# Sigmoid attention and a gated FFN on one core: order of sums in late-sum pairs, place of batch 4's re-laying

## The chip, the cores and the metric

One core of a Trainium2 chip. The time is device microseconds of one execution; the kernel before took a median of 389.58 us in 3 runs (389.45 to 390.1). Engines in the profile: PE is TensorE (PEld its weight loads), DVE is VectorE, ACT is ScalarE, POOL is GpSimd, SP is SyncE, which here issues stores and transposing DMAs.

## The reference, cut to what matters

```python
batch, n_heads, seq, head_dim = (8, 12, 448, 64)
n_tokens, d_model, d_ff = (3584, 768, 1536)

def _attn_ref(q, k, v):
    scores = scale * np.matmul(q, k.transpose(0, 1, 3, 2)) - np.log(S)
    attn = 1.0 / (1.0 + np.exp(-scores))
    return np.matmul(attn, v).astype(np.float32)

def _moe_ref(x, w_gate, w_val, w_out):
    gate = np.maximum(x @ w_gate, 0.0)
    val = x @ w_val
    return (gate * val @ w_out).astype(np.float32)
```

The attention's output, heads side by side (3584 x 768), is the x of the second function; the result is 3584 x 768 in float32. Everything comes in and goes out as float32; the kernel computes in float16 with float32 sums.

## The kernel before, in words

**Attention.** A batch (8 of them, 448 tokens each) has three groups of four heads. k and q of a batch are loaded by POOL's queue with a cast to float16 (`load`, L107), v in three pieces (`load_v`, L113). They are re-laid for the scores: `dma_transposes(b, g)` (L218) makes two copies on VectorE into a tile `rel` (L222, one of k, one of q) and one transposing DMA on SP's queue into `qkT` (L226). There is one buffer for a batch's k and one for its q, so the next batch's loads wait until the last of these copies has read them.

A **score unit** (`qk_unit`, L299) is four 64x64 matmuls of 448 columns that run beside each other (L239) into two PSUM banks, and two sigmoids on ScalarE (L187) into `PT`. Seven units make a group; then `pv_group` (L307, matmuls L257) multiplies them with v into two banks, and `put_xT` writes the result to `xT` on VectorE (L184).

**FFN.** Two batches make a group g of 896 tokens. Gate and value of a pair of 128-wide feature blocks come from `gv_pair` (L588): the Strassen-Winograd scheme with seven products (six matmuls of 448 columns each, L380) in place of eight. The order on TensorE is b, c, b, a, b, c, b, where b is bank pair "u", c "g2", a "g1". VectorE and ScalarE take the partial results out: a first copy of b (L628, by `first_copy`, one copy for each of two banks), `copy` of c and b on ScalarE (L614), `plus` on VectorE (L618), and the gating (L623). A product that adds to a bank whose earlier value is still to be copied has to wait for that copy. The weight sums of the next pair (`unit_sums`, L555) and the sums of x (`batch_sums`, L580) are VectorE's work too. The down projection of two 128-token tiles is `down_pair` (L443), again seven products, of 384 columns, with `token_sums` (L419, four VectorE operations of 128x768) for each pair. `FRESH` and `SUMS_LATE` name pairs whose last token sums are made late: (1, 0), (1, 1), (2, 0), (2, 1) and (3, 3); these have an order of products of their own, in which the products on the late sums come later. In these pairs, `amid` issues a burst of score units into the middle of the pair, and `then` makes the sums of the next pair.

**Order.** Nothing is scheduled by a tool: each engine works through its instructions in the order of the program text. The loop over b (from L912) issues bursts of score units (`burst`, at the places given by `cuts`, with the value product of a group at `pv_at`) and after each burst one pair of FFN work (`next_work`, L887), to which it hands jobs: `ahead` run first, `jobs` inside the pair (`beside`), behind `prepare`, which makes the sums of the next pair. In batch 4 six `gv_pair` of group 1 follow six bursts; in batch 5 come (1, 0), (1, 1), (1, 2); (2, 0) and (2, 1) close batch 7. In batch 4 the first pair (m == 0) also has the sums of x (`batch_sum_steps`) on VectorE, ahead of the first copies and behind the weight sums.

**Banks.** `bank()` (L77) hands out the eight PSUM banks in a ring; `later` (L85) moves some to the ring's end. A matmul into a bank waits until the bank's last reader is done.

Of the kernel before, what the change touches and what calls it, by code (L numbers as in the profile page):

```python
# [18 lines left out]
def kernel(  # L19
# [10 lines left out]
    nc = tc.nc  # L30

    B, H, S, D = q.shape
# [3 lines left out]
    P = 128  # L36
# [48 lines left out]
    def later(order):  # L85
        keys = [free[i - 8] for i in order]
        for key in keys:
            free.remove(key)
            free.append(key)
# [260 lines left out]
    def store(g, t, ysb, m0, m1, engines):  # L350
        for i, eng in enumerate(engines):
            j = 2 * t + i
            b, c = 2 * g + j // NCH, j % NCH
            dst = out[b * S : (b + 1) * S, m0:m1].rearrange("(t c) m -> c t m", c=NCH)[c]
            eng.dma_start(dst, ysb[64 * i : 64 * i + 64, m0:m1])

    HF, HM, HD = NFC // 2, DM // 2, NDC // 2
# [15 lines left out]
    def sums_tile(inner):  # L373
        S3 = late["sums"].tile([P, 3, HF * P], FP16, tag="S", name="S")
        return [S3[:, i, :].rearrange("p (x y) -> p x y", y=inner) for i in range(3)]
# [21 lines left out]
    FRESH = {1: 0, 2: 0, 3: NPP}  # L397
# [21 lines left out]
    def token_sums(g, p, k0=0, k1=HF):  # L419
        for step in token_sum_steps(g, p, k0, k1):  # L420
            step()
# [21 lines left out]
    def down_pair(g, p, beside, then, last, first_copy, amid=None):  # L443
        A11, A12, S3, A22 = token_blocks(g, p)
        S1, S2, S4 = sums.pop(("y", g, p))
        T1, T2, T3, T4 = late["T"]
        B11, B21, B22 = wo[:, 0:HF, 0:HM], wo[:, HF:NFC, 0:HM], wo[:, HF:NFC, HM:DM]
        y1, y2 = (ysbp.tile([P, DM], FP32, tag="ysb", name="ysb") for _ in range(2))
        lo, hi = slice(0, HM), slice(HM, DM)
        b, c = bank("u"), bank("y12")  # L450
        if not amid or (g, p) in SUMS_LATE:
            a = bank("y11")
            later((7, 6, 5))

        def product(ps, A, W, first=True):
            products([(ps, HM, HF, A, W, first)])

        def plus(o, ps):
            nc.vector.scalar_tensor_tensor(  # L459
                out=o, in0=ps[:, 0:HM], scalar=OUT_SCALE, in1=o, op0=AOP.mult, op1=AOP.add  # L460
            )

        first, second = tiles_in(g, p)

        product(b, A11, B11)
        first_copy(y1[:, lo], b)
        beside()
        if (g, p) in SUMS_LATE:
            product(a, A12, B21)
            plus(y1[:, lo], a)  # L470
            product(c, S1, T1)
            scaled_act(y2[:, hi], c)
            product(b, S2, T2, False)
            scaled_act(y1[:, hi], b)
            product(c, S4, B22, False)
            plus(y1[:, hi], c)
            store(*first, y1, 0, DM, (nc.sync, nc.sync))
            if amid:
                amid()
                then()  # L480
            product(b, S3, T3, False)
            plus(y2[:, hi], b)
            scaled_act(y2[:, lo], b)
            d = bank("y21")
            if amid:
                later((0, 7))
            else:
                then()
            product(d, A22, T4)
            plus(y2[:, lo], d)  # L490
            store(*second, y2, 0, DM, (nc.sync, nc.sync))
            return
        product(c, S1, T1)
        scaled_act(y2[:, hi], c)
        product(b, S2, T2, False)
        scaled_act(y1[:, hi], b)
        if amid:
            product(c, S4, B22, False)
            plus(y1[:, hi], c)
            amid()  # L500
            product(b, S3, T3, False)
            plus(y2[:, hi], b)
            later((0,))
            a = bank("y11")
            later((6,))
            product(a, A12, B21)
            plus(y1[:, lo], a)
        else:
            product(a, A12, B21)
            plus(y1[:, lo], a)  # L510
            if last:
                store(*first, y1, 0, HM, (nc.sync, nc.sync))
            product(b, S3, T3, False)
            plus(y2[:, hi], b)
            if last:
                scaled_act(y2[:, lo], b)
                store(*second, y2, HM, DM, (nc.sync, nc.scalar))
            product(c, S4, B22, False)
            plus(y1[:, hi], c)
        if last:  # L520
            store(*first, y1, HM, DM, (nc.sync, nc.scalar))
        else:
            store(*first, y1, 0, DM, (nc.sync, nc.sync))
        then()
        if last:
            for m0 in (0, HM // 2):
                m1 = m0 + HM // 2
                d = bank("y21")
                products([(d, HM // 2, HF, A22, T4[:, :, m0:m1], True)])
                nc.vector.scalar_tensor_tensor(  # L530
                    out=y2[:, m0:m1], in0=d[:, 0 : HM // 2], scalar=OUT_SCALE, in1=y2[:, m0:m1],
                    op0=AOP.mult, op1=AOP.add,
                )
            store(*second, y2, 0, HM, (nc.sync, nc.scalar))
        else:
            product(b, A22, T4, False)
            scaled_act(y2[:, lo], b)
            store(*second, y2, 0, DM, (nc.sync, nc.sync))
# [13 lines left out]
        yield lambda: gate_sums(f, f + 2)  # L552
        yield from unit_sum_steps(("s", f), f, views)

    def unit_sums(key, f):  # L555
        for step in unit_sum_steps(key, f, sums_tile(2 * P)):
            step()

    def unit_sum_steps(key, f, tiles):
        S1, S2, S4 = tiles  # L560
        fs = slice(f * P, (f + 2) * P)
        A11, A12 = wg[:, 0:HD, fs], wg[:, HD:NDC, fs]
        S3, A22 = wv[:, 0:HD, fs], wv[:, HD:NDC, fs]
        sums[key] = S1, S2, S4
        return (
            lambda: sub(S2, A22, S3),
            lambda: nc.vector.tensor_tensor(out=S1, in0=S2, in1=A11, op=AOP.add),
            lambda: sub(S4, A12, S2),
        )
# [18 lines left out]
    def gv_pair(g, f, beside, first_copy):  # L588
# [3 lines left out]
        b, c, a = ([bank(nm) for _ in range(2)] for nm in ("u", "g2", "g1"))  # L592
# [16 lines left out]
            for u in range(2):  # L609
                products([(ps[u], S, HD, sets[u][i], W, first)])  # L610

        def copy(i, ps, by=nc.scalar.copy):
            for u in range(2):
                by(gs[u][i][:], ps[u][:, 0:S])  # L614

        def plus(i, ps):
            for u in range(2):
# [7 lines left out]
            )  # L625

        product(b, 0, B11)
        copy(0, b, first_copy)  # L628
        product(c, 3, T1)
        copy(2, c)  # L630
        product(b, 4, T2, False)
# [243 lines left out]
            tail.insert(NPP if g == 1 else 0, ("y", g, NPP))  # L875
        work.extend(tail)

    def prepare():
        if work:
            kind, g, i = work[0]  # L880
            if kind == "w":
                unit_sums(("w", g, i), i)
            elif kind == "y":
                if (g, i) != (0, 0):
                    token_sums(g, i, 0, HF - 2 if FRESH.get(g) == i else HF)

    def next_work(jobs=(), alone=False, amid=None, ahead=()):  # L887
        kind, g, i = work.popleft()

        due = pending[:]  # L890
        del pending[:]

        def beside():
            for job in due + list(jobs):
                job()

        for job in ahead:
            job()
        if kind == "y":
            down_pair(g, i, beside, prepare, not work, scaled_act if alone else scaled, amid)  # L900
        elif amid:
            raise ValueError(kind)
        elif kind == "w":
            gv_pair(g, i, lambda: (prepare(), beside()), nc.scalar.copy if alone else nc.vector.tensor_copy)
        elif kind == "s":
            gv_split(g, i, lambda: (prepare(), beside()))
        else:
            gv(g, 0, S, i, True)
            beside()
            prepare()  # L910

    for b in range(1, B):  # L912
        if b == 1:
            cuts, pv_at = (0, 3, 6, 9, 13, 17, 21), {3: (0, 2), 5: (1, 2)}
        else:
            cuts, pv_at = (0, 4, 7, 11, 14, 18, 21), {0: (-1, 1 if b == 4 else 2), 2: (0, 2), 4: (1, 2)}
        bursts = list(range(len(cuts) - 1))
        inner = {}
        if b > 2:
# [31 lines left out]
        for m in range(count):  # L951
            jobs, ahead = [], []
            burst(bursts[m])
            if m == 0 and b > 3:
                jobs.append(lambda: dma_transposes(b, 2))
            if b == 2 and m == 3:
                jobs += [lambda: dma_transposes(3, 0), lambda: dma_transposes(3, 1)]
# [7 lines left out]
            if b == 1:  # L965
                if m == 0:
                    load(2, 0, 1, "kq")
                    load(2, 1, 2, "kq")
                    load(2, 2, 3, "kq")
            elif m == 0 and b + 1 < B:  # L970
                for g0, g1 in ((0, 1), (1, NG)) if b == 3 else ((0, NG),) if b > 3 else ():
                    jobs.append(lambda g0=g0, g1=g1: load(b + 1, g0, g1, "kq"))
                jobs.append(lambda: load_v(b + 1))
# [70 lines left out]
```

## Time and profile before

| | |
|---|---|
| median of 3 runs | 389.58 us (389.45 to 390.1) |
| profiled execution | 390.02 us, span of its instructions 388.1 us |
| PE busy | 381.9 us, 98% |
| DVE busy | 303.3 us, 78% |
| ACT busy | 228.5 us, 59% |
| POOL busy | 49.8 us, 13% |
| granted TensorE clock | 1.000 |

The span runs from the first to the last instruction; the 1.92 us beside it lie outside. Rows of the time order have the start in us from the span's start, the length, the engine, line and operation, output and input, size and count; a bracket at the end gives idle time ahead of the row and what ended it. Rows of equal instructions are merged, and a row's length runs from the start of its first to the end of its last. Each burst of units is a row of `qk_ps` (x4 for one unit), a value product is `pv_ps` x28, a product of an FFN pair x6.

### The profile page before, as it was taken

How to read it: one execution, taken by the hardware profiler on the slowest of the kernel's cores; microseconds unless marked ns; L12 is line 12 of the kernel's file. 1: busy time of each engine (PE TensorE's matmuls, PEld its weight loads, DVE VectorE, ACT ScalarE, POOL GpSimd, SP SyncE). 2: the span in 40 equal slices, each digit the busy share in tenths (PEclk: the TensorE clock that was granted, in tenths of full speed). 3: DMA queues.
4: the chain of work that ended last, by engine and by line, in shares of the span. 5: the costliest groups of instructions: out<-in, count | busy, mean ns of one | idle time of the engine just before them, and what ended most of it. 6: DMA issues, size and time to landing. Idle time of an engine off the chain costs nothing.

```text
span 388.1 us, 8975 instructions
## 1 busy us (share of the span) xinstructions
PE 381.9 (98%) x3570; PEld 224.7 (58%) x3570; DVE 303.3 (78%) x606; ACT 228.5 (59%) x483; POOL 49.8 (13%) x73
## 2 busy tenths in 40 slices
PE   8999999999999999999999999999999999999995
PEld 6678776885555545445555554545455555555663
DVE  3455667769868999999857789999987788999563
ACT  5967887567777545455778764545477344333321
POOL 9543306100400210000300300000000000000000
PEclk9999999999999999999999999999999999999999
DMA  9999999999979395022499893222012220000335
GB/s 171 199 199 204 204 188 161 208 208 132 185 162 177 94 160 90 2 49 47 48 228 225 156 231 59 47 50 50 0 41 66 72 72 0 2 0 0 83 90 156
DMA packets 67451, 43.81 MB, mean 113 GB/s; under 512 B 35664, under 2 KB 64080, under 8 KB 67408
## 3 DMA queue, kind: packets, MB, share of 16 engines
q0 software_dynamic: 28960, 23.24, 39.4%
q1 hardware_dynamic: 37664, 19.24, 24.2%
q10 hardware_dynamic: 784, 0.75, 0.6%
q8 instruction: 28, 0.46, 0.5%
q14 instruction: 15, 0.12, 0.1%
HBM read 47.19 MB, written 11.01 MB: 150 GB/s over the span
## 4 chain that ended last, share of the span: by engine, by line
PE 91%; DVE 4%; ACT 3%; issue 1%; DVEq 0%; ACTq 0%
PE u L380 32%; PE g L380 15%; PE y L380 11%; PE qk_ps L239 8%; PE pv_ps L257 7%; PE g_ps L322 5%; PE v_ps L322 5%; ACT PT L187 3%; PE u L701 2%; PE g L701 2%; PE warm_ps L175 1%; PE trt L204 1%; DVE S L371 1%; DVE ysb L459 1%; DVE gsb L618 0%
## 5 line engine op out<-in xcount | busy, mean ns | idle before, releaser
L187 ACT ACTIVATE PT<-qk_ps 128x448 f16<-128x448 f32 (+3 forms) x318 | 151.0, 585 | 79.9 <-PE qk_ps L239 79.8
L380 PEld LDWEIGHTS <-S 128*128 128x128 f16 x576 | 56.3, 98 | 45.9
L618 DVE TENSOR_TENSOR gsb<-g,gsb 128x448 f32<-128x448 f32 x72 | 42.8, 624 | 8.3 <-PE g L380 8.0
L239 PE MATMUL qk_ps<-qkT 64*64 64x448 f16 (+2 forms) x756 | 47.8, 337 | 0.5 <-ACT PT L187 0.3
L380 PEld LDWEIGHTS <-hT 128*128 128x128 f16 x318 | 29.7, 98 | 23.7 <-issue 5.6
L614 ACT COPY gsb<-u 128x448 f32<-128x448 f32 x48 | 25.6, 555 | 23.9 <-PE u L380 22.9
L257 PE MATMUL pv_ps<-PT,v 64*64 64x448 f16 (+2 forms) x756 | 37.0, 329 | 0.0
L459 DVE SCALAR_TENSOR_TENSOR ysb<-y,ysb 128x384 f32<-128x384 f32 x33 | 18.4, 557 | 22.7 <-PE y L380 14.3
L441 ACT ACTIVATE ysb<-u 128x384 f32<-128x384 f32 x32 | 15.7, 491 | 31.5 <-PE u L380 26.8
L184 DVE TENSOR_SCALAR xT<-pv_ps 128x448 f16<-128x448 f32 (+2 forms) x53 | 27.8, 567 | 7.6 <-PE pv_ps L257 6.3
L380 PEld LDWEIGHTS <-wg 128*128 128x128 f16 x216 | 20.3, 98 | 21.9 <-issue 4.1
L380 PEld LDWEIGHTS <-wv 128*128 128x128 f16 x216 | 21.1, 98 | 20.0 <-issue 0.3
L239 PEld LDWEIGHTS <-qkT 64*64 64x64 f16 x756 | 18.1, 106 | 21.1 <-issue 15.0
L380 PE MATMUL u<-wo,hT 128*128 128x384 f16 x156 | 29.8, 327 | 0.2
L111 POOL DMA_DIRECT2D k<-in_k_dram x14 | 10.8, 775 | 142.8 <-DVE rel L222 136.8
L257 PEld LDWEIGHTS <-v 64*64 64x64 f16 x756 | 22.5, 107 | 10.3 <-issue 1.2
L380 PE MATMUL u<-xT,wg 128*128 128x448 f16 x108 | 23.5, 353 | 0.3
L380 PE MATMUL u<-X,wv 128*128 128x448 f16 x108 | 23.4, 352 | 0.1
L380 PE MATMUL u<-X,S 128*128 128x448 f16 x108 | 23.4, 353 | 0.0
L380 PE MATMUL g<-xT,wg 128*128 128x448 f16 x108 | 23.4, 353 | 0.0
L380 PE MATMUL g<-X,S 128*128 128x448 f16 x108 | 23.4, 353 | 0.0
L380 PE MATMUL u<-xT,wv 128*128 128x448 f16 x108 | 23.4, 353 | 0.0
(97 smaller groups left out, 558.8 us busy)
## 6 DMA issues: line engine op xcount, KB each, us to landing
out_dram<-ysb SPq DMA_DIRECT2D x52, 192.0 KB, 3.0
v<-in_v_dram POOLq DMA_DIRECT2D x8, 336.0 KB, 14.9
v<-in_v_dram POOLq DMA_DIRECT2D x16, 168.0 KB, 14.8
k<-in_k_dram POOLq DMA_DIRECT2D x4, 672.0 KB, 11.7
q<-in_q_dram POOLq DMA_DIRECT2D x4, 672.0 KB, 15.0
wo<-in_moe_w_out_dram POOLq DMA_DIRECT2D x2, 1152.0 KB, 19.1
k<-in_k_dram POOLq DMA_DIRECT2D x9, 224.0 KB, 12.0
q<-in_q_dram POOLq DMA_DIRECT2D x7, 224.0 KB, 12.3
```

Of the source, the lines that this page charges most:

```text
L111: nc.gpsimd.dma_start(t16[:, xs, cs], rows_of(src, b)[:, xs, cs])
L184: nc.vector.tensor_scalar(out=xT, in0=src, scalar1=XSCALE, scalar2=None, op0=AOP.mult)
L187: nc.scalar.activation(PT_ap, ps_ap, AF.Sigmoid, bias=sig_bias, scale=qk_scale)
L239: nc.tensor.matmul(out_of(hh)[o : o + 64, :], qkT[rows, c, cols], qkT[rows, NCH + c0 : NCH + c1, cols], start=True, stop=True, tile_positi ...
L257: nc.tensor.matmul(ps[hh][64 * r : 64 * r + 64, 0:qn], v16[rows, 2 * g + hh, c * D : (c + 1) * D], pieces[c][rows, hh, :], start=(c == 0), ...
L322: nc.tensor.matmul(ps[:, 0:qn], (wg, wv)[i][:, dc, f * P : (f + 1) * P], xT_tiles[b][:, dc, q0 : q0 + qn], start=(dc == 0), stop=(dc == ND ...
L380: nc.tensor.matmul(ps[:, 0:n], A[:, k_, :], W[:, k_, :], start=(first and k_ == 0), stop=(k_ == kn - 1), skip_group_check=True,)
L441: nc.scalar.activation(o, ps[:, 0:HM], AF.Copy, scale=OUT_SCALE)
L459: nc.vector.scalar_tensor_tensor(out=o, in0=ps[:, 0:HM], scalar=OUT_SCALE, in1=o, op0=AOP.mult, op1=AOP.add)
L614: by(gs[u][i][:], ps[u][:, 0:S])
L618: nc.vector.tensor_tensor(out=gs[u][i][:], in0=ps[u][:, 0:S], in1=gs[u][i][:], op=AOP.add)
L701: nc.tensor.matmul(ps[j // 2][:, j % 2 * SQ : (j % 2 + 1) * SQ], sets[j][i][:, k_, :], W[:, k_, :], start=(first and j % 2 == 0 and k_ == ...
```

## The change

Four things, all on the order of work; no operation is added or taken out.

1. In the late-sum pairs with `amid` (the first four of `SUMS_LATE`), VectorE makes two of the next pair's four token sums ahead of its read of the product on S3 (`plus(y2[:, hi], b)`) and the other two behind it; before, all four were ahead. TensorE's and ScalarE's order stay.
2. In batch 4's first burst the value product of batch 3's last group follows two score units, before it followed one.
3. In batch 4, `dma_transposes(4, 2)` (two VectorE copies and one DMA on SP) and the loads of batch 5 (k, q and three pieces of v on POOL) are jobs of the third pair (m == 2); before, of the first (m == 0).
4. The first copies of a `gv_pair` can go to two engines: VectorE takes the first, and ScalarE the second, where `ahead` has jobs, which among these pairs is batch 4's first alone. Elsewhere both stay where they were.

```diff
@@ down_pair, SUMS_LATE
+            steps = ()
             if amid:
                 amid()
-                then()
+                steps = prepare_steps()
+                for step in steps[:2]:
+                    step()
             product(b, S3, T3, False)
             plus(y2[:, hi], b)
             scaled_act(y2[:, lo], b)
             d = bank("y21")
             if amid:
                 later((0, 7))
+                for step in steps[2:]:
+                    step()
             else:
                 then()
@@ gv_pair
         product(b, 0, B11)
-        copy(0, b, first_copy)
+        for u in range(2):
+            first_copy[u](gs[u][0][:], b[u][:, 0:S])
         product(c, 3, T1)
@@ prepare
-    def prepare():
+    def prepare_steps():
         if work:
             kind, g, i = work[0]
             if kind == "w":
-                unit_sums(("w", g, i), i)
-            elif kind == "y":
-                if (g, i) != (0, 0):
-                    token_sums(g, i, 0, HF - 2 if FRESH.get(g) == i else HF)
+                return unit_sum_steps(("w", g, i), i, sums_tile(2 * P))
+            if kind == "y" and (g, i) != (0, 0):
+                return token_sum_steps(g, i, 0, HF - 2 if FRESH.get(g) == i else HF)
+        return ()
+
+    def prepare():
+        for step in prepare_steps():
+            step()
@@ next_work
-            gv_pair(g, i, lambda: (prepare(), beside()), nc.scalar.copy if alone else nc.vector.tensor_copy)
+            by = (nc.vector.tensor_copy, nc.scalar.copy)
+            gv_pair(g, i, lambda: (prepare(), beside()), (by[alone], by[alone or bool(ahead)]))
@@ the loop over b
-            cuts, pv_at = (0, 4, 7, 11, 14, 18, 21), {0: (-1, 1 if b == 4 else 2), 2: (0, 2), 4: (1, 2)}
+            cuts, pv_at = (0, 4, 7, 11, 14, 18, 21), {0: (-1, 2), 2: (0, 2), 4: (1, 2)}
...
-            if m == 0 and b > 3:
+            if m == (2 if b == 4 else 0) and b > 3:
                 jobs.append(lambda: dma_transposes(b, 2))
...
-            elif m == 0 and b + 1 < B:
+            elif m == (2 if b == 4 else 0) and b + 1 < B:
                 for g0, g1 in ((0, 1), (1, NG)) if b == 3 else ((0, NG),) if b > 3 else ():
                     jobs.append(lambda g0=g0, g1=g1: load(b + 1, g0, g1, "kq"))
                 jobs.append(lambda: load_v(b + 1))
```

More of the change, by code (lines that the diff above doesn't have):

```diff
@@ L553, in early_sum_steps @@
         yield from unit_sum_steps(("s", f), f, views)
-    def unit_sums(key, f):
-        for step in unit_sum_steps(key, f, sums_tile(2 * P)):
-            step()
     def unit_sum_steps(key, f, tiles):
@@ L610, in product, with copy @@
                 products([(ps[u], S, HD, sets[u][i], W, first)])
-        def copy(i, ps, by=nc.scalar.copy):
+        def copy(i, ps):
             for u in range(2):
-                by(gs[u][i][:], ps[u][:, 0:S])
+                nc.scalar.copy(gs[u][i][:], ps[u][:, 0:S])
         def plus(i, ps):
```

## The prediction, made before the changed kernel ran

> **What bounds the kernel now.** I read the page's busy line first, then batch 4's first pair in the view of stretches (columns: length, then busy time and count of PE, PEld, DVE, ACT, POOL, granted clock, DMA share, GB/s).
>
> ```profile
> PE 381.9 (98%) x3570; PEld 224.7 (58%) x3570; DVE 303.3 (78%) x606; ACT 228.5 (59%) x483; POOL 49.8 (13%) x73
> ...
> 125.80:137.40 11.60, 11.23 (x100) 5.75 (x100) 10.97 (x23) 6.36 (x15) 3.67 (x5) 1.00 0.49 98
> ```
>
> TensorE is busy 98%, at a granted clock of 1.00, so no part of the change can win more than TensorE now loses, and lost time has to be found between the starts of matmul groups: the records overlap (six matmuls whose successors start 1.13 us behind them are shown as 1.30 us long, below), so a short wait hides under the tail of a record. VectorE at 10.97 of 11.60 us in the first stretch is the engine to suspect there. By the busy column the first stretch would have 11.60 - 11.23 = 0.37 us to win; by starts it is 0.65, and I go by starts. The Trainium skill ("Perfetto Trace Analysis", Identifying the Most-Contended Engine) holds that matmul busy time is a poor measure of what is left, because matmuls are pipelined; the two numbers above bear it out.
>
> TensorE in time order, first two undisturbed bursts, then the disturbed places. The columns are start, length, instruction, count.
>
> ```profile
> 155.66 0.76 PE L239 MATMUL qk_ps<-qkT 64*64 64x448 f16 x12
> 156.35 1.31 PE L380 MATMUL u<-xT,wg 128*128 128x448 f16 x6
> 215.40 0.55 PE L239 MATMUL qk_ps<-qkT 64*64 64x448 f16 x8
> 215.88 1.15 PE L380 MATMUL u<-wo,odd 128*128 128x384 f16 x6
> ...
> 127.31 0.74 PE L239 MATMUL qk_ps<-qkT 64*64 64x448 f16 x12
> 128.19 1.29 PE L380 MATMUL u<-xT,wg 128*128 128x448 f16 x6
> ...
> 132.73 1.30 PE L380 MATMUL u<-xT,wv 128*128 128x448 f16 x6
> 133.86 1.30 PE L380 MATMUL g<-xT,S 128*128 128x448 f16 x6
> 135.24 1.30 PE L380 MATMUL u<-X,wv 128*128 128x448 f16 x6
> 136.47 0.76 PE L239 MATMUL qk_ps<-qkT 64*64 64x448 f16 x12
> 137.37 1.29 PE L380 MATMUL u<-xT,wg 128*128 128x448 f16 x6
> ...
> 195.06 0.68 PE L239 MATMUL qk_ps<-qkT 64*64 64x448 f16 x8
> 195.79 0.97 PE L380 MATMUL u<-wo,hT 128*128 128x384 f16 x5
> ...
> 292.27 0.68 PE L239 MATMUL qk_ps<-qkT 64*64 64x448 f16 x8
> 293.00 1.14 PE L380 MATMUL u<-wo,hT 128*128 128x384 f16 x6
> ```
>
> Undisturbed, six 448-column matmuls take 133.86 - 132.73 = 1.13 us from start to start, three score units (x12) with the switch to the next product 0.69, two (x8) 0.48; the third unit is the 0.2 between them. Against these, batch 4's first pair loses 0.88 - 0.69 = 0.19, say 0.20, ahead of its first product (S1); 1.38 - 1.13 = 0.25 ahead of its last product (S2); and 0.90 - 0.69 = 0.21, say 0.20, behind the next burst (S3). Each of three late-sum pairs, the first and the last of them shown, loses 0.73 - 0.48 = 0.25 us behind the burst that follows it (S4). Everything that the change touches therefore loses 0.65 + 0.75 = **1.40 us**.
>
> **The change part by part.**
>
> ```profile
> 126.26 0.98 ACT L187 ACTIVATE PT<-qk_ps 128x448 f16<-128x448 f32 x2
> 127.77 2.73 ACT L187 ACTIVATE PT<-qk_ps 128x448 f16<-128x448 f32 x6 [0.53 <-PE qk_ps L239]
> 130.33 1.02 ACT L614 COPY gsb<-g 128x448 f32<-128x448 f32 x2
> ...
> 127.51 1.16 DVE L184 TENSOR_SCALAR xT<-pv_ps 128x448 f16<-128x448 f32 x2 [0.53 <-PE pv_ps L257]
> 129.24 1.15 DVE L614 COPY gsb<-u 128x448 f32<-128x448 f32 x2
> 130.31 0.55 DVE L371 TENSOR_TENSOR S<-wv 128x768 f16<-128x768 f16 x1
> 133.21 0.39 DVE L222 COPY rel<-q 128x896 f16<-128x896 f16 x1
> 133.51 1.15 DVE L618 TENSOR_TENSOR gsb<-g,gsb 128x448 f32<-128x448 f32 x2
> 134.57 1.15 DVE L618 TENSOR_TENSOR gsb<-u,gsb 128x448 f32<-128x448 f32 x2
> 136.70 1.15 DVE L623 SCALAR_TENSOR_TENSOR hT<-gsb,u 128x448 f16<-128x448 f32 x2
> ```
>
> (1) **The value product one score unit later** (batch 4, burst 0). The eight banks go round in order: now the pair's first "u" banks are those of the value product, and S1 ends at 128.19 just after the first xT write of VectorE (127.51 + 0.58 = 128.09). With two units ahead of it, the "u" banks are those of the second unit instead, which ScalarE frees: its third sigmoid, at a pitch of some 0.45 us (2.73 / 6), starts near 127.16 and ends near 127.7. TensorE wants the bank at 128.19 - 0.20 = 127.99. S1 goes, with 0.3 us to spare; -0.20. The xT writes start one unit, 0.19 us, later. Next late are the "g" banks, which are the value product's now: free at 128.09 + 0.19 and 0.6 later, wanted one product (1.13) after 127.99. No wait.
>
> (2) **One first copy to ScalarE.** VectorE does two in 130.31 - 129.24 = 1.07 us, so it loses 0.53. ScalarE takes it behind eight sigmoids that now run without the 0.53 us gap: 126.26 + 8 x 0.45 = 129.9, ended by 130.4. Its bank is wanted by the second half of the third product, 127.99 + 2.5 x 1.13 = 130.8. Its other copies move 0.1 to 0.3 us and TensorE wants their banks over 0.5 us after they end. Cost 0; without that cover at most one copy, 0.5 us.
>
> (3) **Re-laying copies out of the first pair.** One takes 133.51 - 133.21 = 0.30 us, the two 0.60 us of VectorE. Together VectorE's sums come 0.19 - 0.53 - 0.60 = -0.94 us, at 133.63 in place of 134.57. That one releases the bank that S2 waits for, at 134.2; TensorE wants it at 133.86 - 0.20 + 1.13 = 134.79. S2 goes: -0.25. The gating that releases S3's bank comes at 135.76, ends 136.34; wanted at 136.47 - 0.45 + 0.69 = 136.71. S3 goes: -0.20. The least spare time of the three is 0.3 us.
>
> (4) **The same two copies, one transpose and five loads in the third pair.** For the copies the trace has the case itself: the fifth pair carries two such copies and the same xT writes.
>
> ```profile
> 151.79 1.19 DVE L618 TENSOR_TENSOR gsb<-g,gsb 128x448 f32<-128x448 f32 x2 [0.69 <-PE g L380]
> ...
> 170.32 0.39 DVE L222 COPY rel<-q 128x896 f16<-128x896 f16 x1
> 170.79 1.19 DVE L618 TENSOR_TENSOR gsb<-g,gsb 128x448 f32<-128x448 f32 x2
> ```
>
> In the third pair VectorE idles 0.69 us ahead of its first sum of products; in the fifth the copies stand in that place, and 0.60 us fits into 0.69. Cost 0; without that gap 0.60 at most. The second copy will start near 151.3 (as far ahead of 151.79 as 170.32 is of 170.79), in the time of this execution; everything there comes 0.65 us earlier, wants and arrivals alike.
>
> ```profile
> L226 SPq DMA_TRANSPOSE qkT<-rel x1: 1570/1570/1570, 133.7 to 133.7; - x1
> DMA to landing us min/median/max: 11.4/11.4/11.4
> ...
> L111 POOL DMA_DIRECT2D q<-in_q_dram x1: 831/831/831, 134.4 to 134.4; - x1
> DMA to landing us min/median/max: 14.6/14.6/14.6
> ...
> 164.40 0.57 PE L239 MATMUL qk_ps<-qkT 64*64 64x448 f16 x8
> ```
>
> SP's transpose starts 133.7 - 133.2 = 0.5 us behind the second copy, so at 151.8, and if it needs 11.4 us again it lands at 163.2; the fifth burst's first score unit reads it at 164.40. Spare: 1.2 us. The q load starts 134.4 - 133.2 = 1.2 behind that copy, at 152.5, lands at 167.1, and VectorE re-lays it at 170.32: spare 3.2. The k load is ahead of it in the queue, the v loads behind serve batch 5. SP has nothing else between the stores before this pair and the next transpose, POOL only these loads. Cost 0, with a bound above in the rivals.
>
> (5) **Late-sum pairs.**
>
> ```profile
> 191.28 1.15 PE L380 MATMUL u<-wo,hT 128*128 128x384 f16 x6
> ...
> 191.82 0.56 DVE L371 TENSOR_TENSOR S<-S,hT 128x768 f16<-128x768 f16 x1
> 193.36 0.55 DVE L459 SCALAR_TENSOR_TENSOR ysb<-u,ysb 128x384 f32<-128x384 f32 x1
> ...
> 191.07 2.73 ACT L187 ACTIVATE PT<-qk_ps 128x448 f16<-128x448 f32 x6 [0.86 <-PE qk_ps L239]
> 193.94 0.49 ACT L441 ACTIVATE ysb<-u 128x384 f32<-128x384 f32 x1
> ```
>
> The product ends at 191.28 + 1.15 = 192.43, but VectorE's four sums (they run to 193.4) stand ahead of its read of it; ScalarE reads the same bank only after VectorE has, at 193.94, and the next burst's sigmoids queue behind that. Their third frees the bank of the next "u". With two sums ahead, VectorE reads at about 192.45 and ends at 193.0. Then ScalarE itself is last: a copy stands 130.33 - 127.77 = 2.56 us behind the start of six sigmoids, so here at 193.63, 0.31 us earlier. That covers the 0.25 us by 0.06, so S4 just goes: 3 x 0.25 = -0.75. The two sums that now follow are ready at about 194.0, and the pair that reads them starts at 195.8. The fourth pair ends batch 7: no score units follow it, I enter 0 (other end: 0.25 more).
>
> **Sum.** -0.20 - 0.25 - 0.20 - 0.75 = -1.40 us. The profiled execution took 390.02 us for a span of 388.1; it would give 388.62 (span 386.7). It lies 0.44 above the median of the three runs, 389.58, so I predict 389.58 - 1.40 = **388.2 us**. A measurement of this kernel can tell about 0.2%, 0.8 us, from no change.
>
> **Rivals.**
> - A, slower: **the transpose lands late.** Before, it had four bursts until it was read; after, it has 164.40 - 151.8 = 12.6 us. It decides from a landing above 12.6 us. If the loads held it until the q load is through (167.1), the fifth burst would stand 2.7 us and the time be 389.58 - 1.40 + 2.7 = 390.9. For it: beside the loads it takes 11.4 us already. Against: that is with the very same loads, and nothing else is in flight in the new place. The Trainium skill has a rule that speaks for it ("DMA: Bandwidth & Descriptors", Queues, rings and completion order): each DMA engine takes turns between the queues that have work, packet by packet, so a transpose shares every engine with the loads; it names no bound that 12.6 us would meet. Chance 0.09.
> - B: **ScalarE takes VectorE's place in the late pairs.** If its copy starts only when the sixth sigmoid has ended, 191.07 + 2.73 = 193.80, each pair wins 0.14: 389.58 - 0.65 - 0.42 = 388.5. The 0.06 us of cover speaks for it. Chance 0.14.
> - C: **batch 4's wait is replaced**, by the ScalarE copy or the later xT writes, and only the late pairs win: 389.58 - 0.75 = 388.8. Against it: 0.3 us to spare at each place. Chance 0.11.
> - D: the change does not do what it says, both waits come back in another bank: 389.4. Chance 0.06.
>
> **How the numbers follow.** The forecast has 0.60. Faster by over 0.2% (below 388.8) are the forecast, B and a little of C: 0.75; within 0.2% the rest of C and D: 0.16; slower A: 0.09. The range runs from 387.8 (the fourth pair's 0.25 and some scatter of the runs) to 389.2 (C with the same scatter); outside are A, D and a little at the ends.
>
> **What would show it.** In the profile after: u behind 127.31's burst starts 0.69 us after it, not 0.88; the last product of that pair 1.13 behind the one before; the x8 groups behind the late pairs 0.48 from the next u; ScalarE's ysb copy about 2.56 us behind its six sigmoids; in the third pair no idle time of VectorE; the transpose near 151 landing in 11 to 12 us and no gap of TensorE at the fifth burst. A gap there makes the prediction wrong upward; x8 groups that keep over 0.55 us mean B.

## The result and the profile after

The kernel after took a median of **388.73 us** in 15 runs (388.25 to 389.45), the kernel before 389.58 in 15 runs beside them (389.1 to 390.1): ratio 0.9979, 95% interval 0.9971 to 0.9986. That is 0.85 us won where 1.40 were forecast; 388.73 lies in the range of 387.8 to 389.2, and 0.53 above the 388.2. Its profiled execution took 388.34 us for a span of 386.6.

The busy line of the page after: TensorE shows 1.4 us less of busy time for the same count of instructions. Records overlap, so this is no measure of what was won; the starts below are.

```profile
PE 380.5 (98%) x3570; PEld 224.4 (58%) x3570; DVE 302.6 (78%) x605; ACT 228.4 (59%) x484; POOL 49.5 (13%) x73
```

**How much of the span is the change.** The two profiled executions differ by 1.68 us, twice the medians; their spans differ by 388.1 - 386.6 = 1.5 us, the rest lies outside the spans. The first undisturbed FFN product of batch 3, ahead of every edit, shows where more of it comes from. First the kernel before, then the kernel after, and of each also TensorE's last product:

```profile
66.74 1.32 PE L701 MATMUL u<-xT,wg 128*128 128x224 f16 x12
...
382.99 1.15 PE L380 MATMUL y<-T,hT 128*128 128x192 f16 x12
```

```profile
66.12 1.32 PE L703 MATMUL u<-xT,wg 128*128 128x224 f16 x12
...
381.43 1.15 PE L380 MATMUL y<-T,hT 128*128 128x192 f16 x12
```

The execution after was 0.62 us ahead before it met the first edit (the line numbers differ by two lines that the diff adds). At its last product TensorE is 382.99 - 381.43 = 1.56 us ahead. So the change is worth 1.56 - 0.62 = 0.94 us by these two traces; the medians say 0.85, and 0.94 is inside the interval (0.0014 to 0.0029 of 389.58 is 0.55 to 1.13).

**Batch 4's first pair after.** TensorE in time order:

```profile
126.88 0.55 PE L239 MATMUL qk_ps<-qkT 64*64 64x448 f16 x8
127.36 1.31 PE L380 MATMUL u<-xT,wg 128*128 128x448 f16 x6
...
133.05 1.30 PE L380 MATMUL g<-xT,S 128*128 128x448 f16 x6
134.18 1.30 PE L380 MATMUL u<-X,wv 128*128 128x448 f16 x6
135.41 0.76 PE L239 MATMUL qk_ps<-qkT 64*64 64x448 f16 x12
136.10 1.31 PE L380 MATMUL u<-xT,wg 128*128 128x448 f16 x6
```

Read the differences of starts. Two units to u: 127.36 - 126.88 = 0.48, the undisturbed value. Last product behind the one before: 134.18 - 133.05 = 1.13. Next burst to u: 136.10 - 135.41 = 0.69. All three waits of 0.65 us together are gone. VectorE's sum of products on u, and below it ScalarE, in the same pair:

```profile
133.02 1.14 DVE L619 TENSOR_TENSOR gsb<-u,gsb 128x448 f32<-128x448 f32 x2
```

```profile
125.65 3.59 ACT L187 ACTIVATE PT<-qk_ps 128x448 f16<-128x448 f32 x8
129.06 0.61 ACT L630 COPY gsb<-u 128x448 f32<-128x448 f32 x1
```

ScalarE has one of the two first copies (L630, x1), behind eight sigmoids that run without a gap. VectorE's sum starts at 133.02, before at 134.57: 1.55 earlier, of which 0.62 is the start of the execution, 0.93 the change.

**Batch 4's third pair after.** VectorE; then the transpose (start, and its landing, from the view of the tile rel); then TensorE at the fifth burst:

```profile
150.08 0.38 DVE L222 COPY rel<-q 128x896 f16<-128x896 f16 x1
150.54 1.19 DVE L619 TENSOR_TENSOR gsb<-g,gsb 128x448 f32<-128x448 f32 x2
```

```profile
L226 SPq DMA_TRANSPOSE qkT<-rel x1: 1583/1583/1583, 150.5 to 150.5; - x1
...
DMA to landing us min/median/max: 12.3/12.3/12.3
```

```profile
161.93 1.30 PE L380 MATMUL u<-X,wv 128*128 128x448 f16 x6
163.15 0.57 PE L239 MATMUL qk_ps<-qkT 64*64 64x448 f16 x8
```

The copies (the second of them is shown) have filled VectorE's idle 0.69 us: no bracket is left at the sum. The transpose lands at 150.5 + 12.3 = 162.8, and its reader starts at 163.15, its usual 1.22 behind the product before it: no gap, with 0.35 us to spare and not 1.2.

**A late-sum pair after**, (1, 0): TensorE, ScalarE.

```profile
192.49 1.62 PE L257 MATMUL pv_ps<-PT,v 64*64 64x448 f16 x28
193.82 0.68 PE L239 MATMUL qk_ps<-qkT 64*64 64x448 f16 x8
194.43 1.15 PE L380 MATMUL u<-wo,hT 128*128 128x384 f16 x6
```

```profile
189.83 2.73 ACT L187 ACTIVATE PT<-qk_ps 128x448 f16<-128x448 f32 x6 [0.86 <-PE qk_ps L239]
192.39 0.55 ACT L441 ACTIVATE ysb<-u 128x384 f32<-128x384 f32 x1
```

VectorE now reads u with two sums less ahead of it, at 191.22, and ScalarE's copy stands 192.39 - 189.83 = 2.56 us behind its sigmoids, the number forecast to the hundredth. Yet the units lie 194.43 - 193.82 = **0.61 us** ahead of u, not 0.48: of the 0.25 us only 0.12 went. The pairs (1, 1) and (2, 0) show the same 0.61.

### The profile page after: what moved, and what is told of

The parts are those of the page before. It is cut to its first block, busy times and chain, and to the rows that moved or that the text cites. A ratio compares the mean times of both kernels' runs of the same rounds, so it can differ in the third digit from the quotient of the medians.

```text
span 386.6 us, 8976 instructions
## 1 busy us (share of the span) xinstructions
PE 380.5 (98%) x3570; PEld 224.4 (58%) x3570; DVE 302.6 (78%) x605; ACT 228.4 (59%) x484; POOL 49.5 (13%) x73
## 4 chain that ended last, share of the span: by engine, by line
PE 96%; ACT 2%; DMA 1%; DVE 0%; issue 0%
PE u L380 35%; PE g L380 16%; PE y L380 12%; PE qk_ps L239 10%; PE pv_ps L257 8%; PE g_ps L322 5%; PE v_ps L322 5%; PE u L703 2%; PE g L703 2%; ACT PT L187 2%; PE trt L204 1%; DMA ysb<-in_k_dram 1%; DVE qkT L211 0%; PE warm_ps L175 0%; DVE k L773 0%; DVE ysb L535 0%
## 5 line engine op out<-in xcount | busy, mean ns | idle before, releaser
L257 PEld LDWEIGHTS <-v 64*64 64x64 f16 x756 | 22.5, 107 | 10.3 <-issue 1.1
L380 PE MATMUL g<-xT,S 128*128 128x448 f16 x108 | 23.4, 352 | 0.0
## 6 DMA issues: line engine op xcount, KB each, us to landing
k<-in_k_dram POOLq DMA_DIRECT2D x4, 672.0 KB, 12.2
q<-in_q_dram POOLq DMA_DIRECT2D x7, 224.0 KB, 12.2
```

The lines of the kernel that those rows point to most:

```text
L257: nc.tensor.matmul(ps[hh][64 * r : 64 * r + 64, 0:qn], v16[rows, 2 * g + hh, c * D : (c + 1) * D], pieces[c][rows, hh, :], start=(c == 0), ...
L380: nc.tensor.matmul(ps[:, 0:n], A[:, k_, :], W[:, k_, :], start=(first and k_ == 0), stop=(k_ == kn - 1), skip_group_check=True,)
```

## The experiments

Each diff is against the kernel after; what is left out of a line or between lines is marked by "...". Two theories at first. **M** (mis-sized): batch 4 won its 0.65 in full and each of three late pairs 0.12, the rest being a wait that the prediction didn't see. **W**: the late pairs won 0.75, and batch 4 little, the transpose's late landing having cost the rest.

### The late-sum part alone

```diff
-            gv_pair(..., (by[alone], by[alone or bool(ahead)]))
+            gv_pair(..., (by[alone], by[alone]))
-            cuts, pv_at = ..., {0: (-1, 2), ...}
+            cuts, pv_at = ..., {0: (-1, 1 if b == 4 else 2), ...}
-            if m == (2 if b == 4 else 0) and b > 3:
+            if m == 0 and b > 3:
-            elif m == (2 if b == 4 else 0) and b + 1 < B:
+            elif m == 0 and b + 1 < B:
```

> The late-sum pairs alone are changed; batch 4 is as before. Theory M (the late pairs win 0.12 us each, three of them, and batch 4 wins 0.65): -0.36 us, ratio to before 0.9991, and in the trace 0.61 us from the last two score units behind a late pair to the next u product, with batch 4's first pair as before (0.88 from its burst to the first product). Rival W (each late pair wins the whole 0.25, and the missing part of the predicted 1.40 us is lost where batch 5's loads and the transpose now stand): -0.75 us, ratio 0.9981.

Measured: 389.39 us (11 runs) beside 389.73 of before (27 runs), ratio 0.9995 (0.9986 to 1.0004), so -0.34 by the medians. TensorE of this kernel:

```profile
194.70 0.68 PE L239 MATMUL qk_ps<-qkT 64*64 64x448 f16 x8
195.31 1.15 PE L380 MATMUL u<-wo,hT 128*128 128x384 f16 x6
```

195.31 - 194.70 = 0.61 again, with nothing else changed. 3 x 0.12 = 0.36 agrees with the 0.34; 0.75 is outside the interval, which is 0.55 won to 0.16 lost. The interval holds no change as well, so that the 0.36 was won rests on the trace.

### Batch 4's part alone

```diff
-                steps = prepare_steps()
-                for step in steps[:2]:
-                    step()
+                steps = ()
+                then()
```

> Batch 4's three moves alone; the late-sum pairs are as before. Theory M: -0.65 us, ratio 0.9983, no gap in batch 4's first pair (0.69 to 0.70 behind three units, 1.13 between products), 0.73 us behind the late pairs. Rival W: the moves win 0.65 in the profiled execution but lose part of it in others, when the transpose lands after the fifth burst: -0.2 us, ratio 0.9995, and a wider spread of the times than before.

Measured: 389.28 us (11 runs), ratio 0.9989 (0.998 to 0.9998), -0.45 by the medians. The interval (-0.08 to -0.78) holds both theories, so the time alone settles nothing; the trace does: all three gaps of batch 4's first pair are gone, and the late pairs stand at 0.73 as before. The two halves give -0.34 and -0.45, together -0.79 beside the 0.85; their intervals are too wide for more than that.

### The re-laying one pair earlier

```diff
-            if m == (2 if b == 4 else 0) and b > 3:
+            if m == (1 if b == 4 else 0) and b > 3:
-            elif m == (2 if b == 4 else 0) and b + 1 < B:
+            elif m == (1 if b == 4 else 0) and b + 1 < B:
```

> The changed kernel, with re-laying copies, transpose and loads in batch 4's second pair in place of the third, so that the transpose has some 9 us more until the fifth burst reads it. In the profile of the changed kernel it landed 12.3 us after its start, at 162.8, and the burst stood at 163.15: 0.36 us to spare. Theory M (spare is enough in nearly all executions): same time as the changed kernel, ratio to before 0.998. Rival W (in many executions it lands late): 0.3 to 0.5 us less than the changed kernel, ratio 0.9965 to 0.997. If VectorE lacks the 0.6 us in the second pair, a gap of TensorE of 0.1 to 0.3 us there, and a ratio of 0.9985.

Measured: 389.0 us (11 runs), ratio 0.9981 (0.9973 to 0.999), beside 0.9979 for the kernel after; W's 0.9965 to 0.997 lies outside the interval. The transpose started at 140.8 and landed after 10.3 us, 12.2 us ahead of its reader at 163.32. Twelve us more of spare time bring nothing that these runs resolve (this profile lost 0.37 us to another transpose, below). The traces say it more directly: of the nine profiles of this study in which the re-laying stands in the third pair, each has the fifth burst at its usual 1.22 to 1.23 behind the product before it, with the transpose landed 0.21 to 0.87 us earlier. So W falls.

### Each edit of batch 4 undone by itself

Three kernels, each the kernel after with one edit back, in one execution each (389.46, 389.17 and 389.19 us beside one of before at 389.3: too few for tenths, so the traces decide).

The value product back behind one unit:

```diff
-            cuts, pv_at = ..., {0: (-1, 2), ...}
+            cuts, pv_at = ..., {0: (-1, 1 if b == 4 else 2), ...}
```

> The changed kernel with batch 4's value product back behind one score unit. By the prediction's steps S1 comes back alone (0.2 us ahead of the first product), since the bank is again freed by VectorE's first xT write; VectorE's other two savings, 1.13 us less, keep S2 and S3 away. Rival: the three gaps hang together on VectorE's backlog, and with 1.13 us less of it none comes back.

```profile
127.50 0.74 PE L239 MATMUL qk_ps<-qkT 64*64 64x448 f16 x12
128.38 1.29 PE L380 MATMUL u<-xT,wg 128*128 128x448 f16 x6
```

0.88 where 0.69 is undisturbed: S1 is back, 0.19 us, and S2 and S3 stay away. This edit bought S1 and nothing else.

The re-laying copies, transpose and loads back in the first pair:

```diff
-            if m == (2 if b == 4 else 0) and b > 3:
+            if m == 0 and b > 3:
-            elif m == (2 if b == 4 else 0) and b + 1 < B:
+            elif m == 0 and b + 1 < B:
```

> The changed kernel with the re-laying copies, the transpose and the loads back in batch 4's first pair. VectorE then comes 0.53 - 0.19 = 0.34 us earlier than before, in place of 0.94. By the prediction's steps S2's bank is free at 134.57 - 0.34 + 0.6 = 134.83 and wanted at 134.79 (times of the kernel before): about 0.05 to 0.1 us of gap left. S3's gating would end 136.95 against 136.71 wanted: about 0.2 us of gap left. So of the 0.65 some 0.35 us stay won. Transpose and loads land as before, 11 to 12 us and 14 to 16.

```profile
133.47 1.30 PE L380 MATMUL g<-xT,S 128*128 128x448 f16 x6
134.71 1.29 PE L380 MATMUL u<-X,wv 128*128 128x448 f16 x6
135.94 0.76 PE L239 MATMUL qk_ps<-qkT 64*64 64x448 f16 x12
136.83 1.29 PE L380 MATMUL u<-xT,wg 128*128 128x448 f16 x6
```

The second first copy back on VectorE:

```diff
-            gv_pair(..., (by[alone], by[alone or bool(ahead)]))
+            gv_pair(..., (by[alone], by[alone]))
```

> The changed kernel with both first copies of batch 4's first pair on VectorE. VectorE then comes 0.19 - 0.60 = -0.41 us earlier than before in place of -0.94. By the prediction's steps: S2's bank free at 134.76, wanted 134.79, gap 0 to 0.1 us; S3's gating ends at 136.87, wanted 136.71, gap 0.15 to 0.2 us; none at S1. The second copy of VectorE ends near 130.6 against 130.8 wanted, no gap there. Rival: the copy was not needed, all gaps stay away.

```profile
135.93 0.76 PE L239 MATMUL qk_ps<-qkT 64*64 64x448 f16 x12
136.83 1.30 PE L380 MATMUL u<-xT,wg 128*128 128x448 f16 x6
```

With 0.60 us of copies back, S2 is 1.24 - 1.13 = 0.11 and S3 0.89 - 0.69 = 0.20; with 0.53 us back S3 is 0.90 - 0.69 = 0.21, and its last product stands 1.17 behind the one before, S2 0.04. Either edit alone leaves S3 whole and most of S2 gone; it took both to clear VectorE's lateness at both places. That is what spare times of 0.59 us (134.2 against 134.79) and 0.37 (136.34 against 136.71) in the prediction mean when 0.5 to 0.6 us come back; by the 0.04 and 0.11 that showed, S2's 0.59 was some 0.1 too large.

### What holds the late pairs at 0.61

**L**: the wait is the value product's. Its banks come free in ring order, the second by the sixth sigmoid of the inner burst, and that one ends at 189.83 + 2.73 = 192.56, while the value product starts at 192.49; in the trace one of its matmuls waits for ScalarE and starts at 192.60, 0.11 us behind the first. **B** (the prediction's rival): ScalarE's ysb copy stands ahead of the sigmoid that frees u's bank.

Against B: that copy to VectorE.

```diff
-            scaled_act(y2[:, lo], b)
+            (scaled if amid else scaled_act)(y2[:, lo], b)
```

> The changed kernel, with the late-sum pairs' copy of u behind the inner burst on VectorE in place of ScalarE, so that ScalarE's next eight sigmoids start about 0.37 us earlier while the inner burst's six sigmoids stay where they are. Theory L (the sixth sigmoid of the inner burst frees the value product's second bank): nothing changes on TensorE, value product 1.62 us long, 0.61 us from the last two units to the next u product. Rival B of the prediction (ScalarE's queue: the third of the eight sigmoids frees the u bank): 0.48 us in place of 0.61.

ScalarE, then TensorE:

```profile
190.58 6.42 ACT L187 ACTIVATE PT<-qk_ps 128x448 f16<-128x448 f32 x14 [0.86 <-PE qk_ps L239]
```

```profile
194.57 0.68 PE L239 MATMUL qk_ps<-qkT 64*64 64x448 f16 x8
195.18 1.15 PE L380 MATMUL u<-wo,hT 128*128 128x384 f16 x6
```

and further on

```profile
213.62 0.57 PE L239 MATMUL qk_ps<-qkT 64*64 64x448 f16 x8 [0.58 <-DMA qkT<-rel]
```

Fourteen sigmoids now run in one piece, nothing between them, and it is still 195.18 - 194.57 = 0.61: B's mechanism is out. The one time of this kernel, 389.75, is no argument: the burst at 213.62 comes 0.65 us later than its usual 1.07 behind the product before it, and waits for another transpose (below).

For L: the inner burst one product earlier, so that its sixth sigmoid ends earlier.

```diff
+            if amid:
+                amid()
             product(c, S4, B22, False)
             plus(y1[:, hi], c)
             store(*first, y1, 0, DM, (nc.sync, nc.sync))
             steps = ()
             if amid:
-                amid()
                 steps = prepare_steps()
```

> The changed kernel, with the inner burst of score units of the four late-sum pairs one product (six matmuls of 384 columns, 0.98 us) earlier. Theory L (what ends last behind a late pair is now the sixth sigmoid of the inner burst, which frees the value product's second bank 0.1 us too late, so that its two halves run apart to the end of the burst): the sixth sigmoid ends some 0.9 us earlier, the value product's row is 1.49 us long in place of 1.62, the next u product starts 0.48 us behind the last two units in place of 0.61; three times 0.13 us less than the changed kernel, ratio to before about 0.997. If the units in their new place wait for a bank of the pair's own sums, a gap of up to 0.5 us inside the pair and a ratio of 0.998 to 0.999.

ScalarE, VectorE's read of the pair's last product, then TensorE:

```profile
189.12 2.72 ACT L187 ACTIVATE PT<-qk_ps 128x448 f16<-128x448 f32 x6
```

```profile
193.51 0.55 DVE L459 SCALAR_TENSOR_TENSOR ysb<-y,ysb 128x384 f32<-128x384 f32 x1
```

```profile
192.75 1.49 PE L257 MATMUL pv_ps<-PT,v 64*64 64x448 f16 x28
194.08 0.61 PE L239 MATMUL qk_ps<-qkT 64*64 64x448 f16 x8
194.62 1.15 PE L380 MATMUL u<-wo,hT 128*128 128x384 f16 x6
```

Measured: 388.4 us (5 runs, 388.16 to 388.51), ratio 0.9966 (0.9954 to 0.9979). The sixth sigmoid ends at 191.84, 0.9 ahead of the value product, whose row falls from 1.62 to 1.49 us, and the units lie 0.54 ahead of u. The matmul that waited for ScalarE starts 0.01 us behind the first. L holds. Of the 0.13 us, 0.06 stay, which was not expected. VectorE's read of the pair's last product ends at 193.51 + 0.55 = 194.06, behind two sums ahead of the read of u and two more behind it, and the units start at 194.08: in the trace one of their matmuls waits for VectorE and starts 0.04 us behind the first. With one sum ahead of the read of u, one behind it, and the last two behind the read of the last product:

```diff
+            if amid:
+                amid()
             product(c, S4, B22, False)
...
-                amid()
                 steps = prepare_steps()
-                for step in steps[:2]:
+                for step in steps[:1]:
...
-                for step in steps[2:]:
+                for step in steps[1:2]:
...
             plus(y2[:, lo], d)
+            for step in steps[2:]:
+                step()
```

> The kernel after with the inner burst of the late-sum pairs one product earlier (as in the run before this one of that kind) and only one token sum, in place of two, ahead of the read of the product on S3, the second behind that read, the last two behind the read of the pair's last product. Theory L (what is left behind these pairs is the bank of the value product's or the u product's second half, freed late): VectorE reads that product near 191.65 in place of 192.11, ScalarE's copy starts 0.46 earlier, the last product's bank is read 0.9 earlier, and from the burst's second two units to u it is 0.48 us in place of 0.54: 3 x 0.06 = 0.2 below the 388.4 of the kernel with the burst earlier alone, 388.2, ratio to the kernel before 0.996. Rival (the last 0.06 is a cost of changing from the packed value product to units and no wait): it stays at 0.54, and the time at 388.4.

VectorE's read of the last product, then TensorE:

```profile
192.54 0.56 DVE L459 SCALAR_TENSOR_TENSOR ysb<-y,ysb 128x384 f32<-128x384 f32 x1
```

```profile
193.99 0.55 PE L239 MATMUL qk_ps<-qkT 64*64 64x448 f16 x8
194.47 1.15 PE L380 MATMUL u<-wo,hT 128*128 128x384 f16 x6
```

The read ends at 193.10, 0.9 us ahead of the units, and they lie 0.48 ahead of u: nothing is left of S4. So the 0.25 us were three waits, of 0.12, 0.07 and 0.06, each hidden by the one before. The time, 388.37 us (8 runs, 387.95 to 389.52; ratio 0.9966, 0.9954 to 0.9978), doesn't tell this kernel from the one before it; its profiled execution lost 0.8 us at 212.93, again to that other transpose.

### The price of a late transpose (rival A)

```diff
-            if m == (2 if b == 4 else 0) and b > 3:
+            if m == (3 if b == 4 else 0) and b > 3:
-            elif m == (2 if b == 4 else 0) and b + 1 < B:
+            elif m == (3 if b == 4 else 0) and b + 1 < B:
```

> The kernel after with the re-laying copies, the transpose and the loads of batch 5 in batch 4's fourth pair in place of its third. Prices rival A of the prediction. Theory (the transpose needs 12.3 us wherever these five loads follow it, and nothing hides a late landing): copies near 159.0, transpose issued near 159.6, landed near 171.9; the fifth burst's first unit, at 163.15 in the kernel after, stands until then: a gap of TensorE of 8.7 us, time 388.7 + 8.7 = 397.4. VectorE and the q load give nothing more, since they move by the same amount. Rival (the slow landing belongs to the old places, where stores or other loads are near): it lands in 5 us or less, near 164.6, and the gap is 1.5 us, time 390.2.

Measured: 397.15 us in one execution, 8.42 above the median after. TensorE, then the granted clock in stretches (PEclk stands ahead of the last two columns):

```profile
162.32 1.30 PE L380 MATMUL u<-X,wv 128*128 128x448 f16 x6
170.14 0.96 PE L239 MATMUL qk_ps<-qkT 64*64 64x448 f16 x8 [6.52 <-DMA qkT<-rel]
...
174.16 1.31 PE L380 MATMUL u<-xT,wg 128*128 128x448 f16 x6
```

```profile
163.60:167.00 3.40, 0.02 (x1) 0.00 (x0) 1.75 (x4) 0.00 (x0) 0.00 (x0) 1.00 1.30 169
167.10:173.50 6.40, 3.36 (x36) 1.62 (x40) 0.00 (x0) 1.85 (x4) 0.00 (x0) 0.50 1.27 201
174.00:175.00 1.00, 1.00 (x13) 0.48 (x6) 0.97 (x3) 0.85 (x2) 0.00 (x0) 1.00 0.74 117
```

The total came out near the expected 8.7, by another sum. The transpose landed after 10.2 us, not 12.3, and the burst stood for 170.14 - (162.32 + 1.22) = 6.6 us. The rest, 1.8 us, is clock: the burst and the value product took 174.16 - 170.14 = 4.02 us where the kernel after takes 0.41 + 1.32 + 0.48 = 2.21, at a granted clock of 0.50. TensorE's last record ahead of the wait ends at 162.32 + 1.30 = 163.62, the clock is 1.00 up to 167.0 and 0.50 from 167.1: some 3.4 us into the wait it fell. It is 0.50 up to 173.5 and 1.00 again from 174.0, 3.4 to 3.9 us after work began at 170.14. The Trainium skill ("TensorE: Matmul & The Clock Gate", What's actually happening) says so: half the clock after an idle window of about 3.4 us, the full clock after as long a busy one; the trace agrees with both.

### The transpose for (6, 0)

Gaps of TensorE at the first burst of batch 6 showed up in single profiles: 0.15 us in the kernel with the first copies back, 0.37 in the one with the re-laying one pair earlier, 0.65 in the one with the copy on VectorE, 0.80 in the one with one sum, none in before and after. The reader of that transpose, made in batch 5's last pair, comes 5.3 us behind its start, and it landed after 5.4, 5.65, 5.8 and 6.1 us in these four, after 4.9 and 5.1 in before and after. That the change moves it over that edge is not shown: the landing scatters between profiles by more than the distance to the edge. I tried to take it away, with the first head group of batch 6 loaded and re-laid first:

```diff
-                jobs += [lambda: dma_transposes(6, 0), lambda: dma_transposes(6, 1)]
+                ahead.append(lambda: dma_transposes(6, 0))
+                jobs.append(lambda: dma_transposes(6, 1))
-                for g0, g1 in ((0, 1), (1, NG)) if b == 3 else ...
+                for g0, g1 in ((0, 1), (1, NG)) if b in (3, 5) else ...
```

> The kernel after with one edit in batch 5: k and q of batch 6 are loaded with the first head group ahead of the two others, and the copies and the transpose for (6, 0) run ahead of the pair (1, 2) and not inside it. Theory (the scatter of some executions comes from this transpose, 4.8 to 5.8 us of landing against 5.3 us to its first reader; three of ten profiles show a gap of 0.16, 0.38 and 0.65 us there): the transpose starts 1 us earlier, no profile shows the gap, and since the first group's load is through long before, VectorE does not wait: median 0.1 us below the kernel after, ratio about 0.9975, and the slow end of its runs below 389.2. Rival (the scatter is that of the start, or the extra loads delay other transposes): same median, same spread, or slower by what the split loads cost, 0.2 to 0.5.

Measured: 388.98 us (10 runs, 388.64 to 389.81), ratio 0.9979 (0.997 to 0.9988): no better than after. The transpose started at 206.1 in place of 206.9 (1.0 us earlier once the executions are lined up), as meant, but landed after 6.5 us; TensorE still stood 0.22 us. The theory that an earlier start is enough has fallen. With the earlier inner burst and the order of sums of the kernel with one sum added to it:

> The two edits of the runs before in one kernel: the inner burst earlier with one token sum ahead, and the first head group of batch 6 loaded and re-laid first. Theory: the gains add, 388.2 - 0.1 = 388.1, ratio to the kernel before 0.996. Rival: the earlier copies on VectorE and the changed burst meet in the pair (1, 2) and cost 0.2, ratio 0.997.

Measured: 388.5 us (5 runs, 388.39 to 388.66), ratio 0.9964 (0.9953 to 0.9976). No gap in this profile, but both kernels with split loads show TensorE's weight loads standing 0.31 us near 368, in the down projection at the end. The profile shows nothing that they waited for; the cause is open. The three best kernels (0.9966, 0.9966, 0.9964) can't be told apart. Each beats the kernel before; that they beat the kernel after is not shown by the times, since their intervals overlap its 0.9971 to 0.9986 and they did not run beside it.

## Why the prediction was right, and where its size was off

- **S1, S2, S3 (0.65 us) right, step by step.** Each gap is gone. Undoing the value product's move brings back S1 alone; undoing either relief of VectorE brings back S3 and a little of S2, as the shared margins of steps (2) and (3) have it. VectorE's sum on u came 0.93 us earlier against -0.94 forecast. The ScalarE copy cost nothing.
- **The third pair right, its margin too large.** The distance from the transpose to its reader was forecast as 12.6 us and is 163.15 - 150.53 = 12.62; the landing was put at 11.4, from the one row of the old place, and took 12.3. In the old place it was 11.2 to 11.6 in three profiles, in the third pair 11.8 to 12.4 in nine, in the second 10.3 and in the fourth 10.2 in one each. Rival A didn't happen, by 0.35 us in this profile and 0.21 in the tightest. What makes the landing longer in the third pair is not shown. A's price, the late time itself, would hold for the 2.7 us that it put in, since the clock held for 3.4 us above; the wait of 6.6 us cost 1.8 us of clock besides.
- **Late-sum pairs: the mis-sized term.** The step was "That covers the 0.25 us by 0.06, so S4 just goes: 3 x 0.25 = -0.75". ScalarE came just as early as it said, and each pair won 0.12, so 0.36. The step took one wait to be the whole 0.25, because that wait ended last. Behind it stood the value product's second bank, and behind that VectorE's read of the pair's last product. The first of these could have been read from the kernel before:

```profile
193.74 1.62 PE L257 MATMUL pv_ps<-PT,v 64*64 64x448 f16 x28
```

and undisturbed

```profile
214.08 1.49 PE L257 MATMUL pv_ps<-PT,v 64*64 64x448 f16 x28
```

  The value product in the late pair is 0.13 us longer than the undisturbed one, though the units behind it start at the usual 1.32: a wait inside it that shows only at the next change to full-size matmuls. The inner burst's sixth sigmoid ended at 191.07 + 2.73 = 193.80, behind the value product's start at 193.74; both rows were in its trace.
- **Rival B** gave 0.14 a pair and 388.5, close to the result, but with a cause that the copy on VectorE rules out: near in size, wrong in mechanism.
- **The range** was met with some luck: its lower end was drawn for the fourth pair and its upper for rival C, neither of which happened, and no rival named a wait behind ScalarE's.
- **The sum.** 0.65 + 0.36 = 1.01 us by the rows, 0.94 with the two traces lined up from the start to TensorE's last product; the medians of 15 runs say 0.85, with 0.55 to 1.13 in the interval. The remaining 0.1 is not resolved by these runs.

## What to carry to other kernels

Where several producers release a chain of buffers, don't book the whole gap for removing the wait that ends last: list every release that the stalled group needs with its own time, and take the gap only down to the next one. Compare each group's row length with an undisturbed one of its kind, not only the starts; a longer row at an unchanged pitch is a wait still unpaid. Where a margin rests on one DMA's landing, take it with the spread of such landings, and keep in mind that a long TensorE wait can cost clock on top, as the one of 6.6 us did here.

## What the runs showed of the hardware

- Matmuls that run beside each other in the array (64x64) can start at their usual pitch while one bank's wait, here about 0.1 us, keeps some of them 0.13 us longer (rows of 1.62 and 1.49 us); this is paid at the next 128x128 product (0.61 us behind two units, and 0.54 once the row is 1.49).
- A DMA transpose of the same size lands after 3.9 to 12.3 us within one execution (18 of them in the kernel after, 5.0 in the median), the longest beside the five loads.
- TensorE's clock stayed at 1.00 for some 3.4 us of a wait of 6.6 us, then fell to 0.50, and was back at 1.00 from 3.4 to 3.9 us after work began again.
- Profiled executions differ before the work under study begins: the same product of batch 3, ahead of every edit, starts between 66.12 and 66.93 us in the 14 profiles. Two profiled executions can't be set against each other without lining them up first.
